# Shift and scale of an adaptive layer norm from eight blocks of 4 KB rows, and one row tile turned by a DMA transpose from the ScalarE queue

## The chip, the cores and the metric

The kernel runs on one core of one Trainium2 chip. The metric is the device time of one execution in microseconds (us). All numbers quoted as "us" without a further word are positions or lengths in the profiled execution, counted from its start; "time" means the measured time of a whole execution, as a median over the runs of a kernel. The profile shows one execution, and positions in single profiles vary: the second megabyte of `w_mod`, for one, landed at 13.25 us in the profile of the kernel before and at 12.33 us in that of r10, which issues the same transfers.

## The reference

A conditioned transformer block: six vectors (shift, scale and gate, twice) come from one condition vector `c`; layer norm, shift and scale, linear attention; then the same again with a gated feed-forward. Everything is bf16. Cut to what matters here:

```python
S, D = 2048, 1024                                   # w_mod is (1024, 6*1024), wqkv (1024, 3*1024)
x = A_x
mod = (silu(c) @ w_mod).reshape(1, 6, 1, -1)
sa, ca, ga, sb, cb, gb = ...                        # six rows of 1024
h = layernorm(x) * (1 + ca) + sa                    # needs shift sa and scale ca: 4 MB of w_mod
x = x + ga * linear_attention(h, wqkv, wo)          # q, k, v = h @ wqkv, ...
h = layernorm(x) * (1 + cb) + sb
return x + gb * ((silu(h @ w_gate) * (h @ w_up)) @ w_down)
```

## The kernel before

The sequence is worked in four parts of 512 rows, each of four row tiles of 128. The change touches only the start: the loads, the computation of `sa` and `1 + ca`, and the first part's K projection. The projections of this kernel take the normalised rows turned (features on partitions) in `hT`; there each feature's shift and scale is one number per partition, so `modulate` is one VectorE instruction for each block of 128 features (`cc`, eight of them).

Loads, all issued by SyncE in this order (1 KB rows for `w_mod`: 512 columns at a time, b = column half, q = 1 scale, 0 shift):

```python
    for st in range(STC - 1):
        load_x(st, nc.sync)                     # row tiles 0..2, 256 KB each
    nc.sync.dma_start(out=c_sb[:], in_=c_v)
    load_mod(0, 1, 0, NB)                       # 1 MB each: scale, then shift, of the first half
    load_mod(0, 0, 0, NB)
    load_k(0)
    load_k(1)
    load_x(STC - 1, nc.sync)                    # row tile 3
    load_k(2)
    load_k(3)
    load_mod(1, 1, 0, NB)                       # the second half comes later
    # ... rest of the second half and of K, then V weights, next rows, Q weights
```

The shift and scale as 64 one-column matmuls for each column half, whose weights are blocks of `w_mod` (the result is already one number per partition):

```python
    def mod_block(b, q, lo, hi):
        for i in range(lo, hi):
            col = q * DC + 4 * b + i
            for j in range(DC):
                mm(mod_ps[:, col:col + 1], lhsT=wme[b][q][:, j, i * P:(i + 1) * P],
                   rhs=scT[:, j:j + 1], start=(j == 0), stop=(j == DC - 1))
        # ... copied from PSUM by VectorE, 1 added to the scale
```

The K stage of the first part. `k_groups` are the eight output blocks (row tile, column half); six accumulators run first and need row tiles 0 to 2 only. `keep_warm(acc, n)` is n matmuls of zeros: fillers, meant to keep the clock of TensorE up (with 11 of them at the very start the clock records of this kernel read full speed from 4.7 us on).

```python
    keep_warm(spare, 11)
    # ...
        mm(mod_ps[:, 0:DC], lhsT=c_sb[:], rhs=ident[0:DC, 0:DC], start=True, stop=True)
        keep_warm(spare, 10)
        # ... Silu, statistics and normalisation of tiles 0..2, PE transposes, fillers
        for lo, hi in ((0, 1), (1, 4)):
            mod_block(0, 0, lo, hi)
            for cc in range(lo, hi):
                modulate(hT, cc, ca1T, saT, 0, H)         # H = 3 tiles
        k_mms(0, gs, accs, 0, 4)                          # six accumulators, first four blocks
        xn3 = ln1_norm(*ln1_stats(0, 3), dve=True)
        pe_transpose_tile(hT, xn3, 3, DC // 2)            # tile 3: eight PE transposes, two copies
        for cc in range(4):
            modulate(hT, cc, ca1T, saT, H, SCW)
        mod_block(1, 1, 0, 4)
        # ... K matmuls and the second half's matvecs in turn
        k_evac(0, gs, accs)
        # ... then v_phase(0)
```

## Time and profile before

| | before |
|---|---|
| time, median of 3 runs | 839.24 us (839.12 to 839.3) |
| TensorE (PE) busy | 829.8 of 836.6 us |
| first K matmul | 14.50 us |
| first V matmul | 31.95 us |
| K stage between them | 17.45 us for 64 matmuls that need about 13.9 |

From the first V matmul on the change alters nothing, and TensorE is busy without a break (829.8 of 836.6 us, at a mean granted clock of 1.000). So the question is when V starts. The first part of the page of the kernel before gives the busy time of each engine, its share of the span, and its instructions:

```profile
span 836.6 us, 11355 instructions
## 1 busy us (share of the span) xinstructions
PE 829.8 (99%) x4701; PEld 380.7 (46%) x4701; DVE 307.6 (37%) x598; ACT 170.1 (20%) x255; POOL 60.9 (7%) x165
...
```

The timeline of the kernel before: start, length, engine, source line, operation, output <- inputs, shapes, how many were merged, and in brackets how long the engine had stood idle and what released it.

```profile
...
10.33 0.95 PE L98 MATMUL mod_ps<-scT,wme 128*128 128x1 bf16 x32 [0.20 <-DMA wme<-in_w_mod_dram]
...
13.30 0.35 PE L98 MATMUL mod_ps<-scT,wme 128*128 128x1 bf16 x8 [0.69 <-DMA wme<-in_w_mod_dram]
...
14.50 5.34 PE L98 MATMUL acc<-wk,hT 128*128 128x512 bf16 x24
...
19.68 0.61 PE L101 MATMUL tp<-ident,xn 128*128 128x128 bf16 x8
...
20.13 0.94 PE L98 MATMUL mod_ps<-scT,wme 128*128 128x1 bf16 x32
...
21.78 0.61 PE L98 MATMUL acc<-wk,hT 128*128 128x512 bf16 x2 [0.71 <-DVE hT L218]
...
31.95 13.98 PE L98 MATMUL acc<-wv,hT 128*128 128x512 bf16 x64
...
```

The K matmuls start 1.2 us after the second megabyte of `w_mod` is there (13.30), and are then interrupted: by the PE transposes of tile 3, by matvecs of the second half, by waits for a modulation. The V line gives the undisturbed pace: 64 matmuls in 13.98 us. The chain of waits of the same kernel (start, length, what) says what the start is made of:

```profile
...
2.98 10.27 DMA wme<-in_w_mod_dram
13.25 0.05 issue
13.30 0.37 PE mod_ps L98 x8
...
```

### The profile page before, as it was taken

To read this page: it belongs to the slowest core of one execution; us is meant where nothing else is said; L and a number is where in the kernel's file an instruction comes from. 1 tells how busy PE (TensorE), PEld (TensorE's weight loads), DVE (VectorE), ACT (ScalarE), POOL (GpSimd) and SP (SyncE) were. 2 spreads that over 40 slices of the span, in tenths; PEclk is the share of its full clock that TensorE was granted. 3 is DMA by queue.
4 is the path that set the end of the run, shared out by engine and by line. 5 is a ranking of instruction groups with operands and counts; after the bars stand their busy time and mean duration, and the time that the engine had idled before them with its cause. 6 is when DMAs were issued, how large, how long until landed. Compare 5 with 4: busy or idle time off the path is not lost.

```text
span 836.6 us, 11355 instructions
## 1 busy us (share of the span) xinstructions
PE 829.8 (99%) x4701; PEld 380.7 (46%) x4701; DVE 307.6 (37%) x598; ACT 170.1 (20%) x255; POOL 60.9 (7%) x165
## 2 busy tenths in 40 slices
PE   8999999999999999999999999999999999999998
PEld 4444444444444444444444444444444444444444
DVE  5755554587413324521111344222114431111122
ACT  3455343334211111101111110111110101111000
POOL 2011211111130001100000010000001100000000
PEclk9999999999999999999999999999999999999999
DMA  9894890029997446337434173672505529710011
GB/s 311 305 253 100 254 213 2 13 68 239 366 243 262 151 151 207 120 99 229 150 102 151 45 221 100 201 239 62 189 1 127 188 69 322 241 60 0 13 64 51
DMA packets 127668, 129.34 MB, mean 155 GB/s; under 512 B 33920, under 2 KB 109184, under 8 KB 127104
## 3 DMA queue, kind: packets, MB, share of 16 engines
q1 hardware_dynamic: 123568, 115.36, 45.7%
q0 software_dynamic: 4048, 13.25, 5.4%
q8 instruction: 37, 0.61, 0.3%
q14 instruction: 15, 0.12, 0.1%
HBM read 108.53 MB, written 12.72 MB: 145 GB/s over the span
## 4 chain that ended last, share of the span: by engine, by line
PE 97%; DMA 1%; DVE 1%; SPq 0%; ACT 0%; issue 0%
PE acc L98 89%; PE a_ps L98 7%; DMA wme<-in_w_mod_dram 1%; PE kvp L98 1%; PE modr L98 0%; PE den L98 0%; PE mod_ps L98 0%; DVE hT L218 0%; SPq L120 0%; DVE wo L528 0%; PE wf L98 0%; DVE pq L273 0%; ACT eb L270 0%; ACT hT L226 0%; PE tp L101 0%
## 5 line engine op out<-in xcount | busy, mean ns | idle before, releaser
L98 PE MATMUL acc<-h2T,wgu 128*128 128x512 bf16 x1792 | 387.6, 379 | 0.0
L98 PEld LDWEIGHTS <-wgu 128*128 128x128 bf16 x1792 | 175.3, 98 | 211.3
L98 PE MATMUL acc<-wd,gu 128*128 128x512 bf16 (+2 forms) x924 | 196.1, 373 | 0.0
L597 DVE TENSOR_TENSOR gu<-acc,e 128x512 bf16<-128x512 f32 x112 | 77.5, 692 | 299.2 <-PE acc L98 296.5
L596 ACT ACTIVATE e<-acc 128x512 f32<-128x512 f32 x112 | 66.9, 597 | 374.8 <-PE acc L98 374.8
L98 PEld LDWEIGHTS <-gu 128*128 128x128 bf16 x924 | 89.3, 98 | 104.4
L98 PEld LDWEIGHTS <-hT 128*128 128x128 bf16 x512 | 49.2, 98 | 60.4 <-DVE hT L218 1.5
L618 DVE TENSOR_TENSOR e<-acc,gb_bc 128x512 f32<-128x512 f32 (+2 forms) x33 | 22.3, 675 | 131.9 <-PE acc L98 131.9
L98 PE MATMUL acc<-wk,hT 128*128 128x512 bf16 x256 | 57.6, 379 | 0.8 <-DVE hT L218 0.7
L98 PE MATMUL a_ps<-wo,pq 128*128 128x512 bf16 x256 | 57.4, 379 | 0.0
L98 PE MATMUL acc<-hT,wq 128*128 128x512 bf16 x256 | 56.8, 379 | 0.0
L98 PE MATMUL acc<-wv,hT 128*128 128x512 bf16 x256 | 55.9, 379 | 0.0
L270 ACT ACTIVATE eb<-acc 128x512 bf16<-128x512 f32 x64 | 37.9, 595 | 66.2 <-PE acc L98 63.1
L215 ACT ACTIVATE xn<-x,nmr,rstd 128x1024 bf16<-128x1024 f32 x16 | 19.8, 1240 | 126.3 <-POOL nmr L213 126.3
L565 POOL DMA_DIRECT2D x_scratch<-x x16 | 9.7, 608 | 418.5 <-DVE x L558 418.5
L98 PEld LDWEIGHTS <-pq 128*128 128x128 bf16 x256 | 25.0, 98 | 30.2
L98 PEld LDWEIGHTS <-wq 128*128 128x128 bf16 x256 | 24.6, 98 | 29.8 <-issue 0.9
L271 DVE TENSOR_SCALAR eb<-eb 128x512 bf16<-128x512 bf16 x64 | 18.4, 292 | 49.0 <-ACT eb L270 49.0
L558 DVE TENSOR_TENSOR x<-a_ps,x_sb 128x512 f32<-128x512 f32 x32 | 22.1, 691 | 7.9 <-PE a_ps L98 7.8
L199 POOL TENSOR_TENSOR rstd<-veps,neg_half 128x1 f32<-128x1 f32 x32 | 17.9, 559 | 75.3 <-DVE veps L197 72.9
L308 ACT CAST v<-acc 128x512 bf16<-128x512 f32 x32 | 18.3, 582 | 23.1 <-PE acc L98 23.0
L621 DVE TENSOR_TENSOR ob<-e,x1r 128x512 bf16<-128x512 f32 (+2 forms) x33 | 22.3, 675 | 1.0
(70 smaller groups left out, 263.1 us busy)
## 6 DMA issues: line engine op xcount, KB each, us to landing
wgu<-in_B_w_gate_dram SPq DMA_DIRECT2D x28, 1024.0 KB, 7.9
wgu<-in_B_w_up_dram SPq DMA_DIRECT2D x28, 1024.0 KB, 8.7
x_sb<-in_A_x_dram SPq DMA_DIRECT2D x32, 256.0 KB, 6.8
wml<-in_w_mod_dram SPq DMA_DIRECT2D x8, 1024.0 KB, 8.7
x_scratch<-x POOLq DMA_DIRECT2D x16, 512.0 KB, 3.0
x1r<-x_scratch SPq DMA_DIRECT2D x31, 256.0 KB, 2.8
wd<-in_B_w_down_dram SPq DMA_DIRECT2D x7, 1024.0 KB, 6.0
rbc<-rden_scratch POOLq DMA_DIRECT2D x16, 256.0 KB, 5.4
```

The source lines that it names most:

```text
L98: return tc.keep_in_program_order(nc.tensor.matmul(out, lhsT=lhsT, rhs=rhs, start=start, stop=stop))
L199: nc.gpsimd.tensor_tensor(out=rstd[:, 0:n], in0=veps[:, 0:n], in1=neg_half[:].to_broadcast([P, n]), op=ALU.pow)
L215: nc.scalar.activation(out=dst, in_=src, func=ACT.Identity, bias=nmr[:], scale=rstd[:, 0:1])
L270: nc.scalar.activation(out=e[:], in_=acc, func=ACT.Exp)
L271: nc.vector.tensor_scalar(out=e[:], in0=e[:], scalar1=1.0, scalar2=PHI_EPS, op0=ALU.min, op1=ALU.add)
L308: nc.scalar.copy(out=v[:, t * D + nb * NB:t * D + (nb + 1) * NB], in_=acc[:])
L558: nc.vector.tensor_tensor(out=x1[:, ns], in0=a_ps[:], in1=x_t[:, ns], op=ALU.add)
L565: nc.gpsimd.dma_start(out=x1_dram[st * P:(st + 1) * P, :], in_=x1[:])
L596: nc.scalar.activation(out=sg[:], in_=ps[0][:], func=ACT.Silu)
L597: gm = nc.vector.tensor_tensor(out=guT[sc][f // GPT][:, f % GPT, :], in0=ps[1][:], in1=sg[:], op=ALU.mult)
L618: nc.vector.tensor_tensor(out=yt, in0=y_ps, in1=gb_bc[:, ns], op=ALU.mult)
L621: nc.vector.tensor_tensor(out=ob, in0=yt, in1=x1r, op=ALU.add)
```

## The change

The intent: read `w_mod` as eight row blocks of 128 rows, 4 KB of each row (shift and scale together), so that each block is one transfer of few long rows. Each block is used as the moving operand of four matmuls with 32 output rows each, meant to run side by side; eight blocks accumulate. The result is a row, repeated over 32 partitions, that VectorE turns in 32 x 32 blocks. The 1 of `1 + ca` is put into the accumulator first. With all 4 MB used before the first K matmul, nothing has to interrupt the K stage, and tile 3 leaves TensorE too: it is turned by a DMA transpose issued from the ScalarE queue. The core of the diff:

```diff
-    load_mod(0, 1, 0, NB)
-    load_mod(0, 0, 0, NB)
-    load_k(0) ...
+    for j in range(DC):
+        (nc.scalar if j == 0 else nc.sync).dma_start(out=wme[j // 2][:, j % 2, :], in_=wm_v[:, j, 0:2 * D])
+    for cc in range(4):
+        load_k(cc)
     load_x(STC - 1, nc.sync)
...
+    def mod_block(j):
+        rows = wme[j // 2][:, j % 2, :].rearrange("p (n r) -> p n r", r=P)
+        for g in range(4):
+            mm(mod_ps[32 * g:32 * g + 32, :], lhsT=sc32[:, j, :], rhs=rows[:, :, 32 * g:32 * g + 32],
+               start=False, stop=(j == DC - 1))
+    def mod_turn(lo, hi):
+        src = mod_ps[:].rearrange("p (q i r) -> p q i r", q=2, r=32)
+        for q in range(2):
+            nc.vector.transpose(out=sca[:, q, lo:hi, :], in_=src[:, q, lo:hi, :])
...
-    keep_warm(spare, 11)
+    keep_warm(spare, 4)
...
-        keep_warm(spare, 10)
+        keep_warm(spare, 2)
+        mod_block(0)
+        keep_warm(spare, 2)
+        turn(0)                      # PE transposes of row tile 0
+        mod_block(1)
+        keep_warm(spare, 2)
+        turn(1)
+        mod_block(2)
+        keep_warm(spare, 1)
+        turn(2)
+        mod_block(3)
+        for j, n in ((4, 3), (5, 4), (6, 4), (7, 4)):
+            keep_warm(spare, n)
+            mod_block(j)
+        keep_warm(spare, 4)
+        mod_turn(0, 1)               # ... modulate, mod_turn(1, DC), modulate
+        k_mms(0, gs, accs, 0, 6)
+        xn3 = ln1_norm(*ln1_stats(0, 3))
+        nc.scalar.dma_start_transpose(hT[:, :, H:SCW], xn3[:])
+        for cc in range(DC):
+            modulate(hT, cc, ca1T, saT, H, SCW)
+        k_mms(0, gs, accs, 6, DC)
+        k_mms(0, gs7, accs7)         # the seventh accumulator needs tile 3
```

More of the change, by code (lines that the diff above doesn't have):

```diff
@@ L121, in load_x @@
         x_tiles[st] = x_sb
-    for st in range(STC - 1):
-        load_x(st, nc.sync)
-    nc.sync.dma_start(out=c_sb[:], in_=c_v)
+    load_x(0, nc.sync)
+    load_x(1, nc.scalar)
+    load_x(2, nc.sync)
+    nc.scalar.dma_start(out=c_sb[:], in_=c_v)
     wk = [big("wk", [4, D]), big("wk", [4, D])]
-    wme = [[big("wme", [DC, NB]) for _ in range(2)] for _ in range(2)]
-    def load_mod(b, q, lo, hi):
-        nc.sync.dma_start(out=wme[b][q][:, :, lo:hi], in_=wm_v[:, :, q * D + b * NB + lo:q * D + b * NB + hi])
+    wme = [big("wme", [2, 2 * D]) for _ in range(DC // 2)]
     def load_k(cc):
         nc.sync.dma_start(out=wk[cc // 4][:, cc % 4, :], in_=wqkv_v[:, cc, D:2 * D])
-    load_mod(0, 1, 0, NB)
-    load_mod(0, 0, 0, NB)
-    load_k(0)
-    load_k(1)
+    for j in range(DC):
+        (nc.scalar if j == 0 else nc.sync).dma_start(out=wme[j // 2][:, j % 2, :], in_=wm_v[:, j, 0:2 * D])
+    for cc in range(4):
+        load_k(cc)
     load_x(STC - 1, nc.sync)
-    load_k(2)
-    load_k(3)
-    load_mod(1, 1, 0, NB)
-    load_mod(1, 0, 0, NB // 2)
-    load_k(4)
-    load_k(5)
-    load_mod(1, 0, NB // 2, NB)
-    load_k(6)
-    load_k(7)
+    for cc in range(4, DC):
+        load_k(cc)
     def load_w(view, lo, name):
@@ L167 @@
     nc.vector.memset(neg_half[:], -0.5)
+    base = ep.tile([P, NB], BF16, name="eb")
+    nc.gpsimd.memset(base[:, 0:NB // 2], 0.0)
+    nc.gpsimd.memset(base[:, NB // 2:], 1.0)
     scT = const.tile([P, DC], BF16, name="scT")
     sc32 = const.tile([P, DC, 32], BF16, name="sc32")
-    saT = const.tile([P, DC], F32, name="saT")
-    ca1T = const.tile([P, DC], F32, name="ca1T")
+    scaT = const.tile([P, 2, DC], F32, name="scaT")
+    saT, ca1T = scaT[:, 0, :], scaT[:, 1, :]
+    sca_t = ep.tile([P, NB], F32, name="e")
+    sca = sca_t[:].rearrange("p (q i r) -> p q i r", q=2, r=32)
+    sa0T, ca0T = sca[:, 0, :, 0], sca[:, 1, :, 0]
     sbT = const.tile([P, DC], F32, name="sbT")
@@ L219, in modulate, with pe_transpose_tile @@
                                 scalar2=biasT[:, cc:cc + 1], op0=ALU.mult, op1=ALU.add)
-    def pe_transpose_tile(hT, xn, t, split):
+    def pe_transpose_tile(xn):
         tp = acc_b("tp", (DC, P), BF16)
@@ L224, in pe_transpose_tile @@
             transpose(tp[:, cc, :], xn[:, cc * P:(cc + 1) * P])
-        if split < DC:
-            nc.scalar.copy(out=hT[:, split:DC, t * P:(t + 1) * P], in_=tp[:, split:DC, :])
-        nc.vector.tensor_copy(out=hT[:, 0:split, t * P:(t + 1) * P], in_=tp[:, 0:split, :])
+        return tp
     hTs = {}
@@ L251, in ln1, with mod_open @@
             ln1_norm(*ln1_stats(sc, t))
-    def mod_block(b, q, lo, hi):
-        for i in range(lo, hi):
-            col = q * DC + 4 * b + i
-            for j in range(DC):
-                mm(mod_ps[:, col:col + 1], lhsT=wme[b][q][:, j, i * P:(i + 1) * P],
-                   rhs=scT[:, j:j + 1], start=(j == 0), stop=(j == DC - 1))
-        cs = slice(4 * b + lo, 4 * b + hi)
-        src = mod_ps[:, q * DC + 4 * b + lo:q * DC + 4 * b + hi]
-        if q == 1:
-            nc.vector.tensor_scalar_add(out=ca1T[:, cs], in0=src, scalar1=1.0)
-        else:
-            nc.vector.tensor_copy(out=saT[:, cs], in_=src)
+    def mod_open():
+        for g in range(4):
+            mm(mod_ps[32 * g:32 * g + 32, :], lhsT=ident[:, 0:32], rhs=base[:], start=True, stop=False)
+    def mod_block(j):
+        rows = wme[j // 2][:, j % 2, :].rearrange("p (n r) -> p n r", r=P)
+        for g in range(4):
+            mm(mod_ps[32 * g:32 * g + 32, :], lhsT=sc32[:, j, :], rhs=rows[:, :, 32 * g:32 * g + 32],
[4 more added lines that the diff above has]
+            nc.vector.transpose(out=sca[:, q, lo:hi, :], in_=src[:, q, lo:hi, :])
     last_phi = [None]
@@ L424 @@
     with in_order(nc.vector, nc.scalar, nc.gpsimd):
+        c_ps = acc_b("mod_ps")
+        mm(c_ps[:, 0:DC], lhsT=c_sb[:], rhs=ident[0:DC, 0:DC], start=True, stop=True)
         mod_ps = acc_b("mod_ps")
-        mm(mod_ps[:, 0:DC], lhsT=c_sb[:], rhs=ident[0:DC, 0:DC], start=True, stop=True)
-        keep_warm(spare, 10)
-        nc.scalar.activation(out=scT[:], in_=mod_ps[:, 0:DC], func=ACT.Silu)
-        xns = [ln1_norm(*ln1_stats(0, t)) for t in range(3)]
-        pe_transpose_tile(hT, xns[0], 0, DC)
@@ L431 @@
-        keep_warm(spare, 3)
-        pe_transpose_tile(hT, xns[1], 1, DC)
-        keep_warm(spare, 2)
-        mod_block(0, 1, 0, 4)
-        pe_transpose_tile(hT, xns[2], 2, DC // 2)
-        keep_warm(spare, 4)
-        for lo, hi in ((0, 1), (1, 4)):
-            mod_block(0, 0, lo, hi)
-            for cc in range(lo, hi):
-                modulate(hT, cc, ca1T, saT, 0, H)
-        k_mms(0, gs, accs, 0, 4)
-        xn3 = ln1_norm(*ln1_stats(0, 3), dve=True)
-        pe_transpose_tile(hT, xn3, 3, DC // 2)
@@ L444, with turn @@
-        for cc in range(4):
+        mod_open()
+        nc.scalar.activation(out=scT[:], in_=c_ps[:, 0:DC], func=ACT.Silu)
+        st0 = ln1_stats(0, 0)
+        nc.vector.tensor_copy(out=sc32[:], in_=scT[:].unsqueeze(2).to_broadcast([P, DC, 32]))
+        xns = [ln1_norm(*st0)] + [ln1_norm(*ln1_stats(0, t)) for t in range(1, 3)]
+        def turn(t):
+            tp = pe_transpose_tile(xns[t])
+            nc.vector.tensor_copy(out=hT[:, :, t * P:(t + 1) * P], in_=tp[:])
+        keep_warm(spare, 2)
@@ new lines @@
+        mod_block(0)
[11 more added lines that the diff above has]
+            mod_block(j)
+        keep_warm(spare, 4)
+        mod_turn(0, 1)
+        modulate(hT, 0, ca0T, sa0T, 0, P)
+        modulate(hT, 0, ca0T, sa0T, P, H)
+        mod_turn(1, DC)
@@ L445 @@
+        for cc in range(1, DC):
+            modulate(hT, cc, ca0T, sa0T, 0, H)
+        nc.vector.tensor_copy(out=scaT[:], in_=sca[:, :, :, 0])
+        k_mms(0, gs, accs, 0, 6)
+        xn3 = ln1_norm(*ln1_stats(0, 3))
+        nc.scalar.dma_start_transpose(hT[:, :, H:SCW], xn3[:])
+        for cc in range(DC):
             modulate(hT, cc, ca1T, saT, H, SCW)
-        mod_block(1, 1, 0, 4)
+        k_mms(0, gs, accs, 6, DC)
         gs7, accs7 = k_groups[6:7], [acc_b("acc")]
-        k_mms(0, gs7, accs7, 0, 2)
@@ L449 @@
-        for cc in (4, 5):
-            mod_block(1, 0, cc - 4, cc - 3)
-            modulate(hT, cc, ca1T, saT)
-            if cc == 4:
-                k_mms(0, gs7, accs7, 2, 4)
-        k_mms(0, gs + gs7, accs + accs7, 4, 5)
-        k_mms(0, gs[0:4], accs[0:4], 5, 6)
-        mod_block(1, 0, 2, 4)
-        for cc in (6, 7):
-            modulate(hT, cc, ca1T, saT)
-        k_mms(0, gs[4:6] + gs7, accs[4:6] + accs7, 5, 6)
-        k_mms(0, gs + gs7, accs + accs7, 6, 8)
+        k_mms(0, gs7, accs7)
@@ L465 @@
         k_evac(0, gs8, accs8)
-    with tc.issue_after(last_on[nc.vector.engine]):
-        nc.vector.tensor_copy(out=sc32[:], in_=scT[:].unsqueeze(2).to_broadcast([P, DC, 32]))
     with tc.issue_after(last_on[nc.gpsimd.engine]):
```

## The prediction

> **What bounds the kernel now.** TensorE: the page has it busy 829.8 of 836.6 us (99%), clock granted in full, and the chain of waits is 97% TensorE. From the first V matmul (31.95 us in the timeline) onwards the change touches nothing. So only the moment at which V starts can move the time. Before it stand 64 K matmuls; in the V stage 64 take 13.98 us, so K needs about 13.9 us. First K matmul: 14.50 us. Thus 14.5 us of start plus 17.45 us of K stage, 3.6 us of which is interruption (mod matvecs, turned tile 3, waits for modulation). In the chain, 10.3 us of the first 14.5 are the shift/scale weights' transfer.
>
> **What is removed.** 256 one-column mod matmuls (32 take 0.94 us), eight PE transposes of tile 3 (0.6 us) and their copies, and the interruptions of the K stage: about 3.6 us of TensorE.
>
> **What is added.** Before any modulation all 4 MB of shift/scale weights must land, not 2 MB. By the first modulation 3 x 256 KB + 4 MB = 4.98 MB have landed instead of 2.9 MB. Transfers ran at 253-316 GB/s in the 1 KB-row stage from 4 to 7 us, and at 390-400 GB/s with 2 KB rows. I expect 4 KB rows at about 385: estimate 0.86 MB by 4.5 us, the rest in 10.7 us, completion and uneven engines 0.5-1: last block at 16.2 us (before, the last needed block landed at 13.25, because some DMA engines ran 2.8 us behind others[...]).
> Then the last four 32-column matmuls (the existing 32 matvecs of this form span about 2 us, so 0.25 us), two small VectorE transposes (no trace has one; estimate 0.2 us each from the 0.16 us copy of a PSUM column), modulation of 128 columns (0.31 us): first K matmul at 17.3 us, 2.8 later than before. Two larger VectorE transposes (0.35-0.4 us each) cost another 0.2. The first six accumulators then run 48 matmuls unbroken to 27.9 us; K ends at 31.3 if tile 3 is ready: a gain of 0.6 us.
>
> **Tile 3.** VectorE finishes seven 384-column modulations (0.38 us each) at 21.2 us; statistics 1.6, POOL 1.1 with gaps, ScalarE normalisation 1.24: 25.2 us. The transpose must also wait for its semaphore slot (the first V weights, about 24.5 us). Existing DMA transposes land 2.7 us after issue when the engines are free (12 of 24 within 3.6), but 7.0-10.5 us where other traffic runs. Here 2 KB weight rows fill the other queue[...]. The trace shows 17 ns per 256 B and 84 ns per 2 KB packet; 64 turns per engine are 6.5 us. I expect landing between 28 and 33.5 us, so TensorE, free at 27.9, waits 0.5 to 6 us. This may eat the gain.
>
> **Sum.** -0.6 us plus a wait centred on 2: V starts 1.3 us later. Predicted 840.5 us, range 836.8 to 846. Chances: faster by over 2% 0.005, within 2% 0.985, slower by over 2% 0.01.
>
> **What would show it.** Timeline: last mod matmul near 16, first K matmul near 17.3, 48 K matmuls unbroken, then a gap on TensorE released by modulation (DVE hT) behind the ScalarE-queue DMA transpose; its issue to landing above 4 us. V start minus 31.95 us equals the change in time.
>
> **What would make it wrong.** 4 KB rows landing by 14.8 us (gain up to 2 us); the transpose landing in 3 us (no wait); a wait[...] dropping the granted TensorE clock, adding 1-2 us; engines still running unevenly.

What no run of this case had shown is cut from the recorded text, and the cuts are marked: the ground given for turns between the DMA queues, a guess about descriptors, and a threshold for the clock. No term of the sum is cut. It came to the first K matmul at 17.3 us, the end of K at 31.3 (0.6 us of gain), and with a wait of 2 us V 1.3 us later (rounded), 840.5 us. The 6.5 us for the transpose of tile 3 are the estimate from two packet times in the trace: 1,024 packets of 256 B on 16 engines are 64 on each, and if each has one 2 KB packet beside it, that is 64 x (17 + 84) ns. That the packets of the two queues go one for one had not been shown then; r3 counts them. Of the other estimates, the VectorE transposes took 0.19 us (two small) and 0.39 us (two larger), as was guessed. The 7.0 to 10.5 us from issue to landing are those of five of the 28 DMA transposes in the kernel before, beside 0.7 to 1.3 MB of other traffic; the shortest took 2.7 us, beside under 0.1 MB.

## The result, and the profile after

| | before | after |
|---|---|---|
| time, median of 4 runs | 839.27 us (839.12 to 839.95) | 850.07 us (848.75 to 851.11) |
| last block of `w_mod` landed | | 15.5 us |
| first K matmul | 14.50 us | 20.89 us |
| first V matmul | 31.95 us | 42.47 us |

The ratio is 1.0126 (95% interval 1.0109 to 1.0144). A ratio here is the mean time of one kernel's runs over that of the other's in the same rounds, so it is not quite the ratio of the medians. The change makes the kernel 10.8 us slower, within the 2% class but well outside the predicted range (836.8 to 846). V starts 10.5 us later: the loss is all ahead of it, as argued, only much larger.

The timeline of the changed kernel (columns as above):

```profile
...
1.74 0.44 ACTq L135 DMA_DIRECT2D wme<-in_w_mod_dram  x1
...
8.88 0.62 PE L98 MATMUL mod_ps<-wme,sc 128*32 128x512 bf16 x4 [4.15 <-DVE stats L202]
...
9.43 1.03 PE L98 MATMUL acc<-sel 128*128 128x512 bf16 x2
...
10.25 1.06 PE L101 MATMUL tp<-ident,xn 128*128 128x128 bf16 x8
...
19.69 0.40 PE L98 MATMUL mod_ps<-wme,sc 128*32 128x512 bf16 x4
...
20.14 0.31 DVE L261 STREAM_TRANSPOSE e<-mod_ps 128x32 f32<-128x32 f32 x2 [4.63 <-PE mod_ps L98]
...
20.89 10.52 PE L98 MATMUL acc<-wk,hT 128*128 128x512 bf16 x47
20.98 0.71 DVE L261 STREAM_TRANSPOSE e<-mod_ps 128x224 f32<-128x224 f32 x2
...
27.85 1.33 ACTq L459 DMA_TRANSPOSE hT<-xn  x1
...
36.83 1.88 DVE L215 TENSOR_SCALAR hT<-hT,scaT 128x128 bf16<-128x128 bf16 x8 [11.29 <-DMA hT<-xn]
...
37.20 5.43 PE L98 MATMUL acc<-wk,hT 128*128 128x512 bf16 x16 [5.79 <-DVE hT L215]
...
42.47 13.98 PE L98 MATMUL acc<-wv,hT 128*128 128x512 bf16 x62
...
```

Two cautions first. The view counts 47 and 62 matmuls where the program has 48 and 64: some matmul records are missing from a trace. And it names a statistics instruction of VectorE as what released TensorE at 8.88 us, but that had merely ended about then; block 0 of `w_mod`, issued on the ScalarE queue at 1.74 us, landed at 8.84 us. The list of transfers (output <- input, queue, kind, count, size, us from issue to landing) has it:

```profile
...
wme<-in_w_mod_dram ACTq DMA_DIRECT2D x1, 512.0 KB, 7.1
...
```

By the packet records its 128 packets of 4 KB moved from 5.1 to 8.3 us, beside 185 packets of the later blocks on the SyncE queue.

Three things are to be read in the timeline. First, the last matvec block ran at 19.69 us, 4.2 us after its data had landed: TensorE worked with only one gap of 0.16 us from 8.88 us on and was behind. Second, 48 K matmuls ran unbroken from 20.89 us in 10.5 us, as intended. Third, TensorE then stood idle 5.79 us until VectorE had modulated tile 3, which VectorE could not do before the DMA transpose landed, and the 16 matmuls after that took 5.43 us where 3.5 is the full-speed time (a quarter of the 13.98 us of the V line). The chain of waits of the changed kernel names the transfer:

```profile
...
26.58 1.25 ACT xn L212
27.83 0.02 issue
27.85 8.96 DMA hT<-xn
36.81 0.03 issue
36.83 0.33 DVE hT L215
...
```

The busy times by stretch (length, then busy us and instructions of each engine, granted TensorE clock, share of the DMA engines, GB/s) show the clock go down with the wait:

```profile
core 0: us, PE busy (x) PEld busy (x) DVE busy (x) ACT busy (x) POOL busy (x), PEclk, DMA share, GB/s
...
5.00:10.00 5.00, 1.12 (x6) 0.49 (x7) 4.06 (x12) 2.48 (x2) 2.19 (x6) 1.00 1.01 411
...
30.00:35.00 5.00, 1.42 (x7) 0.45 (x5) 0.00 (x0) 2.06 (x4) 0.00 (x0) 0.91 1.09 384
35.00:40.00 5.00, 2.79 (x7) 1.07 (x8) 3.10 (x12) 0.27 (x1) 0.00 (x0) 0.50 0.08 14
40.00:45.00 5.00, 4.95 (x21) 2.16 (x21) 4.83 (x11) 2.72 (x6) 0.00 (x0) 0.91 0.01 2
...
```

(For 5 to 10 us the view prints 1.00 as well, but the trace has no clock record there; the length of the matmuls tells: two fillers took 1.03 us at 9.43, and 0.59 at 15.27.)

The transfers themselves got better: 411 GB/s from 5 to 10 us, where the kernel before moved 327. The sum of the shift of V: the first K matmul came 6.4 us later; the interruptions of 3.6 us went; the wait for tile 3 added 5.8 and the half clock after it 1.9. That is 10.5 us.

### The profile page after: what moved, and what is told of

Same layout as the page of the kernel before. It is cut to its first block, busy times and chain, and to the rows that moved or that the text cites. A ratio compares the mean times of both kernels' runs of the same rounds, so it can differ in the third digit from the quotient of the medians. Undisturbed runs are those within 1.5% of the kernel's fastest.

```text
span 847.8 us, 11090 instructions
## 1 busy us (share of the span) xinstructions
PE 828.1 (98%) x4521; PEld 378.9 (45%) x4601; DVE 307.6 (36%) x599; ACT 170.4 (20%) x254; POOL 61.4 (7%) x168
## 3 DMA queue, kind: packets, MB, share of 16 engines
q0 software_dynamic: 4048, 13.25, 5.2%
## 4 chain that ended last, share of the span: by engine, by line
PE 96%; DVE 2%; DMA 1%; issue 1%; ACT 0%; POOL 0%
PE acc L98 87%; PE a_ps L98 6%; DMA hT<-xn 1%; DVE stats L202 1%; PE kvp L98 1%; PE modr L98 0%; DMA x_sb<-in_A_x_dram 0%; PE mod_ps L98 0%; DVE hT L215 0%; PE tp L101 0%; PE den L98 0%; ACT xn L212 0%; DVE wo L530 0%; PE wf L98 0%; DVE e L261 0%
## 5 line engine op out<-in xcount | busy, mean ns | idle before, releaser
L212 ACT ACTIVATE xn<-x_sb,nmr,rstd 128x1024 bf16<-128x1024 bf16 x16 | 19.8, 1240 | 24.5 <-POOL nmr L210 24.4
```

The costliest lines, as they stand in the source:

```text
L212: nc.scalar.activation(out=dst, in_=src, func=ACT.Identity, bias=nmr[:], scale=rstd[:, 0:1])
```

## The experiments

All twelve give the right result. "First K", "V" are the starts of the first K and V matmul in the profiled run, "T" is the DMA transpose of tile 3, from issue to landing. "Pause" is a later break of TensorE between 120 and 140 us that the profile attributes to nothing; it is explained with r9. For orientation, all of them at once:

| run | first K | T | V | pause | time, median | ratio to before (95%) |
|---|---|---|---|---|---|---|
| before | 14.5 | | 31.95 | no | 839.27 | |
| after | 20.9 | 27.85 to 36.81 | 42.5 | no | 850.07 | 1.0126 (1.0109 to 1.0144) |
| r1 | 20.5 | | 34.8 | yes | 843.68 | 1.0060 (1.0044 to 1.0077) |
| r2 | 18.7 | 25.70 to 36.34 | 42.8 | yes | 853.85 | 1.0180 (1.0163 to 1.0198) |
| r3 | 21.2 | 28.11 to 32.22 | 36.1 | yes | 843.44 | 1.0057 (1.0040 to 1.0074) |
| r4 | 20.1 | 27.02 to 36.39 | 41.6 | yes | 849.57 | 1.0137 (1.0118 to 1.0156) |
| r5 | 18.2 | | 32.5 | yes | 841.88 | 1.0042 (1.0026 to 1.0059) |
| r6 | 17.3 | | 31.6 | yes | 840.22 | 1.0020 (1.0006 to 1.0035) |
| r7 | 18.2 | | 32.5 | no | 839.43 | 1.0011 (0.9997 to 1.0026) |
| r8 | 18.0 | 25.00 to 28.60 | 32.5 | yes | 840.05 | 1.0019 (1.0004 to 1.0034) |
| r9 | 17.8 | | 32.0 | no | 839.09 | 1.0015 (1.0003 to 1.0028) |
| r10 | 13.6 | | 31.0 | yes | 839.64 | 1.0026 (1.0012 to 1.0040) |
| r11 | 17.7 | | 32.0 | no | 839.43 | 1.0015 (1.0003 to 1.0028) |
| r12 | 14.2 | 27.81 to 38.45 | 51.3 | no | 857.23 | 1.0210 (1.0193 to 1.0227) |

The kernel before, run beside them, had medians of 838.11 (r1 to r4), 838.18 (r5 to r8), 838.09 (r9 to r11) and 839.17 (r12): the chips and rounds differ by up to 1.2 us, so times of different groups are compared by their ratios.

### r1: tile 3 turned on TensorE again

```diff
-        nc.scalar.dma_start_transpose(hT[:, :, H:SCW], xn3[:])
+        tp3 = pe_transpose_tile(xn3)
+        nc.vector.tensor_copy(out=hT[:, :, H:SCW], in_=tp3[:])
```

> The changed kernel with tile 3 turned on TensorE again (eight 128x128 transposes after the first 36 K matmuls, one VectorE copy). Theory A (the ScalarE-queue DMA transpose is the main loss): the 5.8 us wait of TensorE before the seventh accumulator goes, and so does the half-speed stretch after it (16 K matmuls in 5.4 us instead of 3.5); the transposes cost 0.6 us. V starts near 35.3 us instead of 42.5, and the time is about 842.8 us (842 to 844). Rival B (the late first K matmul, 20.9 instead of 14.5 us, is the main loss and the wait only hides behind it): the time stays above 846 us. Both: the first K matmul stays at 20.9 us within 0.5.

Measured: V at 34.8 us, first K matmul at 20.5, time 843.68 us. From the timeline of r1, TensorE alone:

```profile
...
20.52 7.93 PE L98 MATMUL acc<-wk,hT 128*128 128x512 bf16 x36
28.29 0.61 PE L101 MATMUL tp<-ident,xn 128*128 128x128 bf16 x8
28.74 6.21 PE L98 MATMUL acc<-wk,hT 128*128 128x512 bf16 x28
34.78 10.52 PE L98 MATMUL acc<-wv,hT 128*128 128x512 bf16 x48
```

The DMA transpose cost 7.7 us of V's start: 5.8 of waiting and 1.9 of half clock; the first K matmul 0.4 us earlier and the 0.45 us of PE transposes cancel. Theory A holds. But a loss of 0.6%, about 5 us, remains. Of this 2.8 us are the later start of V, which belongs to the other half of the change; the rest lies behind V, where the profile shows a pause of 0.8 us (see r9) and nothing for what is left.

### r2: the clock up before the first block

```diff
-    keep_warm(spare, 4)
+    keep_warm(spare, 11)
...
-        keep_warm(spare, 2)
+        keep_warm(spare, 12)
         mod_block(0)
```

> The changed kernel with 17 more filler matmuls ahead of the first mod block (11 at the start as before the change, 12 instead of 2 before block 0). Theory C (the first K matmul is late because TensorE sat idle from 4.7 to 8.9 us, ran at half speed until about 13.5 and then worked off its 20 fillers behind data that had landed at 15.5): fillers, turns and blocks take full-speed times from 8.9 us on, and the first K matmul comes at 18 to 18.5 us instead of 20.9. Rival (4 MB must land and be used): it stays within 0.5 of 20.9. For the time: if the transpose of tile 3 takes a fixed 9 us after its issue, V starts 2.6 us earlier (847.4 us); if it lands only when the other queue's backlog is gone (about 35.5 us), V starts at most 1.3 us earlier (849 us).

Measured: the first K matmul came at 18.75 us, 2.1 us earlier, and yet the time rose to 853.85 us. The timeline of r2, TensorE alone, shows two fillers in 0.60 us and eight PE transposes in 0.61, where the changed kernel took 1.03 and 1.06, and then where the gain went:

```profile
...
9.17 0.60 PE L98 MATMUL acc<-sel 128*128 128x512 bf16 x2
9.61 0.61 PE L101 MATMUL tp<-ident,xn 128*128 128x128 bf16 x8
...
18.75 10.52 PE L98 MATMUL acc<-wk,hT 128*128 128x512 bf16 x48
36.74 6.27 PE L98 MATMUL acc<-wk,hT 128*128 128x512 bf16 x16 [7.46 <-DVE hT L215]
42.85 4.48 PE L98 MATMUL acc<-wv,hT 128*128 128x512 bf16 x20
```

So theory C is right about the first K matmul, with 0.3 us missing to the expected value. On the time both forecasts missed: the transpose was issued 2.15 us earlier and landed only 0.5 us earlier, after 10.6 us, so the wait grew to 7.5 us. With the longer wait the clock also stood at half for 10.2 us instead of 6.8 (from the clock records of the traces; the granted clock of r2 was 0.59 from 30 to 40 us and 0.89 from 40 to 50), and the 16 matmuls took 6.3 us, and a pause (2.9 us between two matmul starts at 134.9 us, with the clock at half again from 137.7 to 141.1) came on top. V itself started only 0.4 us later than in the changed kernel; in the two profiles the last matmul came 4.2 us later, so most of r2's loss against the changed kernel lies behind V.

### r3: the other queue held back

```diff
-    wq = load_w(wqkv_v, 0, "wq")          # and the next row tiles, ahead of the K stage
...
+    # behind the K stage of the first part:
+    hold = dram.tile([1, P], BF16, name="hold")
+    nc.sync.dma_start(out=hold[:], in_=hT[0:1, 0, H:SCW])     # waits until tile 3 is turned
+    wq = load_w(wqkv_v, 0, "wq")
```

> The changed kernel with the 2 MB of q weights held back on their queue until tile 3 has been turned (a small transfer that reads tile 3 stands before them). Theory A1 (the transpose is slow because 2 KB weight rows of the other queue take turns with it): it lands 3 to 4.5 us after issue instead of 9.0, TensorE waits under 1 us, no half-speed stretch follows, V starts near 35 us and the time is 842 to 843.5 us. Rival A2 (the transpose from that queue is slow by itself, or came too late for the accumulators anyway): landing stays above 7 us and the time above 848 us.

Measured: 4.1 us from issue to landing instead of 9.0, time 843.44 us. From the timeline of r3:

```profile
...
28.11 1.33 ACTq L455 DMA_TRANSPOSE hT<-xn  x1
...
32.62 3.67 PE L98 MATMUL acc<-wk,hT 128*128 128x512 bf16 x16 [0.94 <-DVE hT L211]
...
36.13 1.24 PE L98 MATMUL acc<-wv,hT 128*128 128x512 bf16 x5
...
```

The wait shrank from 5.79 to 0.94 us and the half clock after it is gone (3.67 us for 16). V started 1.1 us later than expected: 0.94 us of wait were left, and the first K matmul came 0.3 us later than in the changed kernel. Theory A1 holds, if not to the microsecond: it was the traffic of the other queue that made the transpose slow here.

The packet records of the trace show how. This is a count of packets by queue and microsecond, made from the records of the changed kernel (q1 is the SyncE queue, q10 the ScalarE queue):

```
us          q1, 2048 B    q10, 256 B
30 to 31       196             0
31 to 32       193            22
32 to 33       168           168
33 to 34       169           182
34 to 35       108           461
35 to 36        11           173
```

The transpose moves 1,024 packets of 256 B. While both queues had work, about one 2 KB packet of the weights went by for each 256 B packet of the transpose: 168 against 168 from 32 to 33 us, 169 against 182 in the next. So the transpose got half of the packets but one ninth of the bytes. It also began late: its first packet moved 3.9 us after issue, and so it did in r2; in r3 it was 2.1 us, and with little or no other traffic 1.3 us (issue at 42.81 us in the kernel before; r8, below, likewise). What holds the first packet back was not tested.

### r4: the same transpose from the SyncE queue

```diff
-        nc.scalar.dma_start_transpose(hT[:, :, H:SCW], xn3[:])
+        nc.sync.dma_start_transpose(hT[:, :, H:SCW], xn3[:])
```

> The changed kernel with the transpose of tile 3 issued from the SP queue, behind the q weights, instead of the ScalarE queue. If a queue of its own gives the transpose no more than a place at the end of the backlog, it lands at 36 to 37 us as it did (36.8), and the time is 849 to 851 us. If turns between the queues did help it, landing is later than 38 us and the time above 852 us. If the ScalarE queue itself is slow, it lands before 34 us and the time is below 848 us.

Measured: landing at 36.39 us, time 849.57 us, as in the changed kernel. With the Q weights already queued, a queue of its own gained the transpose nothing here over the end of the line (in r4 its first packet moved at 33.1 us, after nearly all of the weights).

### r5 and r6: the start without the transpose

r5 is r1 with the early fillers of r2. r6 also cuts the later fillers:

```diff
         mod_block(0)
-        keep_warm(spare, 2)
         turn(0)
         mod_block(1)
-        keep_warm(spare, 2)
         turn(1)
         mod_block(2)
-        keep_warm(spare, 1)
         turn(2)
         mod_block(3)
-        for j, n in ((4, 3), (5, 4), (6, 4), (7, 4)):
+        for j, n in ((4, 0), (5, 3), (6, 3), (7, 3)):
```

> Tile 3 turned on TensorE (as in r1) and the 17 early fillers of r2. With the wait for the transpose gone, the 2.1 us that r2 gained at the first K matmul must now reach V: first K matmul near 18.6 us (r1: 20.5), V start near 32.9 us (r1: 34.8), time about 1.9 us below that of r1 (841.5 to 842.5 at r1's 843.7). If V does not move with the first K matmul, something else behind it sets V.

> r5 with the fillers behind mod block 0 cut from 20 to 9 (none before block 4, three before each of the last three). Theory C says fillers paced TensorE behind the data: the last block landed at 15.5 us, so the last block runs by 16.0 and the first K matmul comes at 16.9 to 17.2 us, V near 31.3 us, the time 0.3 to 1 us below that of the kernel before. Rival (the matvecs and turns themselves pace it): first K matmul stays above 18 us.

From the timeline of r6, the lines of TensorE for the last block, the first K and the first V matmuls:

```profile
...
16.11 0.40 PE L98 MATMUL mod_ps<-wme,sc 128*32 128x512 bf16 x4
...
17.32 7.93 PE L98 MATMUL acc<-wk,hT 128*128 128x512 bf16 x35
...
31.58 1.67 PE L98 MATMUL acc<-wv,hT 128*128 128x512 bf16 x6
...
```

Measured for r5: first K matmul 18.2, V 32.5 us; with the wait out of the way the earlier start reached V in full (2.3 us), and the ratio fell from 1.0060 to 1.0042, about 1.5 us. For r6: 17.3 and 31.6 us, V 0.4 us ahead of the kernel before, which is less than positions vary between single profiles. Theory C holds: the first K matmul of the changed kernel was 3.6 us later than r6's, 2.3 us of it by the half clock (r1 to r5, 20.5 to 18.2) and 0.9 us by fillers (r5 to r6, 18.2 to 17.3; the split depends on the order, as r7 will show), while 0.4 us lie between two runs of one start (the changed kernel and r1); what is left, 17.3 against 14.5, is the price of waiting for 4 MB. But r6's time did not follow its V: it should have been below that of the kernel before, and was 0.2% above. Something behind V cost about 2 us.

### r7: fewer fillers and no early ones

> r6 without the 17 early fillers: fillers cut, but TensorE at half speed from about 5 to 14 us. If the half-speed start matters only through the backlog, the first K matmul comes within 0.7 us of r6's (below 17.8 us); but with fewer fillers the clock may also still be at half when K starts, and then 48 K matmuls take over 11.5 us instead of 10.5 and the time is 1 to 3 us above r6's.

r6 with the two early `keep_warm` counts back at 4 and 2. Measured: first K matmul 18.2 us, 0.9 later than r6 (expected within 0.7), K at full speed, and the time 0.8 us below r6's although V starts 0.9 us later. The early half clock alone is worth only 0.9 us once the backlog of fillers is gone. So the two causes overlap: taken this way, the fillers are worth 2.3 us (r1 to r7) and the clock 0.9 (r7 to r6); through r5 it is the reverse. And r7 has no pause.

### r8: the transpose kept, its traffic held back, the start of r6

```diff
+    hold = nc.sync.dma_start(out=hold_t[:], in_=hT[0:1, 0, H:SCW])
+    with tc.issue_after(hold.ins):
+        # next row tiles and Q weights only from here on
```

> r6's start with the ScalarE-queue DMA transpose of tile 3 kept, and the next row tiles and the q weights held back until it has landed (the V weights still in flight). Theory A1: issue near 24 us, landing within 5.5 us of issue, a wait of TensorE under 2.5 us ahead of the seventh accumulator, time 0.5 to 3 us above r6's. If the transpose had been worth it without other traffic, the time would be at or below r6's.

Measured: landing 3.6 us after issue, a wait of 0.4 us, V at 32.5 us, 0.9 later than r6. Most of the 0.9 us is the first K matmul, which came 0.7 us later than in r6 (the last block landed at 16.4 us instead of 15.8); from the first K matmul to V r8 took 14.46 us and r6 14.26. Even in the clear the transpose does not beat 0.45 us of PE transposes, though it nearly breaks even: the times, 840.05 and 840.22 us, cannot be told apart.

### r9, r10, r11: the pause

From the timeline of r6, TensorE alone; `kvp` are 128 short matmuls, each with its weight load, in 1.2 us:

```profile
...
122.47 1.22 PE L98 MATMUL kvp<-v,pk 128*32 128x64 bf16 x128
123.85 1.03 PE L98 MATMUL acc<-wk,hT 128*128 128x512 bf16 x4 [0.16 <-issue]
126.12 2.12 PE L98 MATMUL acc<-wk,hT 128*128 128x512 bf16 x9 [1.25 <-issue]
```

"issue" means that no recorded instruction or transfer of data released TensorE. A 16 KB instruction fetch runs from 123.7 to 124.8 us in r6. It was the guess, which no trace shows, that a start that differs by some tens of instructions shifts the place where such fetches fall in the program. r9 tests whether their number matters: the same start with another number of instructions.

```diff
-        keep_warm(spare, 12)
+        keep_warm_narrow(spare, 98)       # 64 columns each instead of 512
```

> r6 with its 12 fillers of 512 columns before block 0 replaced by 98 fillers of 64 columns: the same 2.8 us of TensorE, but 172 more TensorE instructions ahead of everything else, so that every later instruction has the same number as in the kernel before. In r6 TensorE stood still 1.6 us at 124.5 us with no releaser, right after the second burst of 128 kv matmuls pairs and beside a 16 KB instruction fetch; r1, r5, r8 show 1 to 1.7 us there, the kernel before, the changed kernel and r7 none. Theory D (where instruction fetches fall against that burst depends on how many instructions come earlier): the pause is gone, first K matmul and V start stay as in r6 (17.3, 31.6 us) within 0.3, and the time is 1.3 to 1.8 us below r6's, at or up to 0.5 us below the kernel before. Rival (the pause comes from the changed order of transfers): it stays.

> The kernel before with ten 512-column fillers replaced by five of them and 47 of 64 columns: 84 more TensorE instructions early[...]. Theory D: a pause of 1 to 1.7 us appears at 120 to 126 us, V starts at 31.95 us within 0.3, and the time is 1 to 2 us above the kernel before. Rival: no pause, time within 0.4 us of the kernel before.

> r9 with two fillers instead of three before each of blocks 5, 6 and 7 (and three more narrow ones early, so the instruction numbers stay). The last block landed at 15.8 us in r6 and its matmuls ran at 16.1: the first K matmul comes 0.1 to 0.3 us earlier than in r9 and the time falls by as much. If the clock drops for want of fillers, the time rises by 1 us or more.

Measured for r9: no pause. Every later landmark coincides with the kernel before (last matmul at 833.3 us in both). V came 0.4 us later than in r6, since the last block landed at 16.5 us instead of 15.8, and the time is 839.09 us, ratio 1.0015: the expected gain over r6 (1.0020) is not shown, since the intervals overlap, and r9 is not below the kernel before. That it is 0.15% above, although its profile ends as that of the kernel before does, is not explained. For r10, the kernel before with 84 more TensorE instructions early: the pause appears (1.32 us between two matmul starts at 123.9 us, where 0.22 is usual), and the time rose by 1.55 us. From its timeline, TensorE alone:

```profile
...
123.29 1.03 PE L98 MATMUL acc<-wk,hT 128*128 128x512 bf16 x4 [0.16 <-issue]
125.26 1.04 PE L98 MATMUL acc<-wk,hT 128*128 128x512 bf16 x4 [0.94 <-issue]
```

Its V started at 31.0 us, earlier than expected, because in that run the second megabyte of `w_mod` landed at 12.3 us instead of 13.25; the pause ate it. (The profiled run is the fastest of the five.) So the pause comes and goes when the early fillers alone are exchanged, in either kernel and with the transfers in the same order. That it is the fetch that arrives late is likely but not shown. The packet records speak for it: in all eight runs with a pause TensorE went on 1.2 to 1.5 us after the end of a 16 KB instruction fetch. The rule by numbers is also not complete: r3 and r4 paused 1 us, with as many TensorE instructions as the changed kernel, which did not pause. r11 tried two late fillers in place of three: first K matmul at 17.7 us, no gain, no drop of the clock.

### r12: the second part of the change alone, on the kernel before

```diff
-        pe_transpose_tile(hT, xn3, 3, DC // 2)
+        nc.scalar.dma_start_transpose(hT[:, :, H:SCW], xn3[:])
```

> The second part of the change alone, on the kernel before: tile 3 turned by a ScalarE-queue DMA transpose in place of the eight PE transposes, all else as it was. Tile 3 is normalised by 18.7 us, but the transpose takes the semaphore slot of the first V weights and so waits until they have landed (28.3 us), and the other queue stays full until about 40 us. Theory A1 (it lands when that backlog is nearly gone): landing at 36 to 41 us, TensorE waiting from about 21.8 us on because the seventh accumulator needs tile 3 early in this order, the clock falling to half, V starting between 46 and 53 us and the time 852 to 860 us. Rival (a fixed 9 us after the normalisation): landing near 28 us and the time 844 to 848 us.

Measured: issued at 27.81 us, since it shares a semaphore with the first V weights and had to wait until these had landed at 27.74 us, landed at 38.45 us, 10.6 us later; time 857.23 us. The waits of r12 (engine and line, what for, us, times, longest):

```profile
...
PE acc L98 <- DVE hT L218: 18.6, 1, 18.6
...
```

In the order of this kernel the seventh accumulator needs tile 3 from 20.3 us on, so the wait is this long. The first two K matmuls after it took 1.03 us, as two fillers at half clock did in the changed kernel, and the mean granted clock of the run was 0.988. Here the other queue stayed full all the while. From 32 to 37 us the transpose moved 168 to 181 packets in each microsecond beside 162 to 172 of the weights: 1,024 packets at that pace are 6.0 us, and the first moved 3.95 us after issue; 0.7 us passed from the last packet to the semaphore. That is the same 10.6 us as in r2, and it settles what r2 left open: beside a full queue the transpose took 10.6 us from issue in both; in the changed kernel it took 9.0, where the weights ran out at 35 us.

## Why the prediction was wrong

- **V's start decides: right.** V moved by 10.5 us, the time by 10.8.
- **4 KB rows: right, and better than said.** 404 to 426 GB/s from 5 to 13 us where 385 was assumed; the last block landed at 15.5 us (predicted 16.2). That the DMA engines run more evenly for it is not shown: from its first to its last engine the second megabyte took 2.8 us in the kernel before, and the last block 0.75 us in the changed kernel, 0.96 in r6 and 1.75 in r9.
- **"First K matmul at 17.3 us": wrong by 3.6 us.** The step failed on TensorE, which the sum took to be free when the data came. It waited for block 0 until 8.88 us, idle for 4.15 us, stood at half clock (the trace's clock records show full speed from 13.6 us on, in the kernel before from 4.7), and had 20 fillers, three turned tiles and eight blocks to do in order. r6, with the clock up and 9 fillers, started K at 17.3 us, the very number, in part by luck: the last block landed 0.4 us earlier than predicted (15.8 us), and from there to K it took 1.5 us instead of 1.1. r5, r6 and r7 show that the error came of the clock and the fillers.
- **48 K matmuls unbroken, interruptions saved: right.** 10.5 us as predicted. r6 and r9 show the balance of this half of the change: 2.8 to 3.3 us later at the first K matmul, 3.2 saved behind it, V at 31.6 and 32.0 against 31.95 us. The prediction had said 0.6 us of gain, and it is nothing that the times show. (It also speaks of 256 one-column matmuls; the trace has 128. Nothing in its sum hangs on this.)
- **The wait for tile 3: right in kind, mis-sized.** The prediction's own sum of turns, 6.5 us, was right (6.0 measured in r12). But it then let the landing range down to 28 us and centred the wait on 2, although it had itself read 7.0 to 10.5 us from issue to landing where other traffic runs; the 9.0 us here lie within that. It left out that the first packet would move late (3.9 us after issue here, beside a full queue), and the issue was itself 2.6 us later than predicted, since VectorE takes up tile 3 only after the modulations, and those came late with the matvecs. The wait was 5.8 us; r1 removes it and r3 all but 0.9 us of it, in two ways.
- **The half clock after the wait: named as a risk, not in the sum.** The clock records read half speed from 34.1 us, 2.7 us into the wait of 5.8, to 40.9. It cost 1.9 us.
- **Sum.** Predicted shift of V: 1.3 us; measured 10.5. Of the 9.2 us missing, 3.6 are the first K matmul, 3.8 the longer wait, 1.9 the clock (0.1 is rounding). These are not independent: r2 started K 2.1 us earlier and lost it in the wait and the clock. Tile 3 is the step that broke the forecast: without its DMA transpose and with K as late as it was, the time was 843.68 us (r1), inside the predicted range; with K earlier and the transpose kept, it was 853.85 (r2).

No version of the change beat the kernel before: r7 cannot be told from it (0.9997 to 1.0026), and r9 and r11 are slower by 0.03 to 0.28%.

## What to carry to other kernels

The DMA transpose of 1,024 packets of 256 B, beside a full queue of 2 KB rows, paid about one long packet for each short one (168 to 168; 9.0 to 10.6 us from issue to landing, where 2.7 is the shortest in the kernel before), and in the same queue it waited for what stood before it (r4: 9.4 us to landing); put such a transpose on a critical path only where the other traffic has been held back, or leave it to TensorE if that costs half a microsecond (0.45 us in r1). When a stage waits for data piece by piece, add up the in-order engine's own work from its first possible start, fillers and slow clock (1.03 us for two fillers here instead of 0.6) included, and compare that with the landing of the last piece. A gain ahead of a landing that does not move is lost in the wait, and can come back as a loss through the clock (r2: K 2.1 us earlier, V 0.4 us later).
